# Wider GpSimd additions, later stores and later loads of q and k in an attention and feed-forward kernel

## The chip, the cores and the metric

The kernel runs on one core of one Trainium2 chip, in float32. The metric is the time of one execution on the device in microseconds (us), as the median of several executions. Ratios are the mean time of one kernel's fast runs over that of the other's in the same rounds on the same chip, so they are not quite the ratio of the medians that stand beside them. Where a difference in us is given for an experiment, it is the ratio less one, times 1402 us.

Engine names in the profile: PE is TensorE, PEld its weight loads, DVE is VectorE, ACT is ScalarE, POOL is GpSimd, and SPq is the queue of the SyncE engine, which issues nearly all transfers and does so strictly in order.

## The reference

```python
# attention: batch 8, 12 heads, 448 positions, head size 64
q_n, k_n = rmsnorm(q, g_q), rmsnorm(k, g_k)
scores = matmul(q_n, k_n.T) / sqrt(64)
attn   = softmax(scores)                  # row maximum taken off, 1e-9 added to the sum
x      = matmul(attn, v)                  # -> (3584 tokens, 768)
# feed-forward
h = x @ w_in                              # w_in (768, 2048)
g = maximum(h, 0) ** 2
out = g @ w_out                           # w_out (2048, 768)
```

The two weights arrive as float64. The kernel has to turn them into float32 itself.

## The kernel before

The feed-forward products are done with 7 block products instead of 8 (a Strassen-like scheme), so each pair of weight pieces is first turned into seven blocks: A11, A12, A21, A22 and the sums S1 to S4. These are written to scratch memory in HBM (`w1s`, `w2s`) and read again as blocks `sw` by the products. The two batches that come first have no feed-forward beside them; in this part (`attention_alone`, up to about 134 us) the weights are converted in between. Only this part and the first product after it (134 to 265 us) are touched by the change.

A weight piece goes through one "tick" of four steps. ScalarE and VectorE make the float32 exponent, GpSimd adds the mantissa to it as an integer (`value`) and makes the sums (`total`), and the queue stores the seven blocks:

```python
A11, S2, S1, S3, A12, A22, S4 = range(7)
A21 = 7

def prepare(t):                                  # t: number of the weight piece
    def value(n, half):
        to = ((A11, A12), (A21, A22)) if n < NFC else ((A11, A21), (A12, A22))
        dst = blocks_of(n)[:, to[n % 2][half]]   # 128 x 384
        ...
        nc.gpsimd.tensor_tensor(*[x.bitcast(I32) for x in (dst, low[:, part], eu[:, part])], ALU.add)
    def total(n, dst, x, y, op):
        if there(n) and n % 2:
            nc.gpsimd.tensor_tensor(*[blocks_of(n)[:, i] for i in (dst, x, y)], op)
    ...
    n = t - 3
    if there(n) and n % 2:                       # the store, in the first step
        nc.sync.dma_start(dst.rearrange("k p m -> p k m"), blocks_of(n)[:, 0:7])
    ...
    yield
    ...                                          # second step: ScalarE, VectorE
    yield
    nc.vector.scalar_tensor_tensor(eu, high, 0xC0000000, bits, ALU.bitwise_and, ALU.bitwise_or)
    total(t - 2, S3, A11, A21, ALU.subtract)
    total(t - 2, S4, A12, S2, ALU.subtract)
    value(t - 1, 0)
    yield
    unsigned(t + 1)
    value(t - 1, 1)
    total(t - 1, S1, A21, A22, ALU.add)
    total(t - 1, S2, S1, A11, ALU.subtract)
    load_words(t, t - 1)
    yield
```

One pair of heads in the attention. `norm` squares q and k on ScalarE, sums on VectorE, takes the power -1/2 on GpSimd and multiplies q on GpSimd; `transpose` turns q and k on TensorE; `add_up` adds two tiles of probabilities on VectorE:

```python
def add_up(i, c):
    acc = acc_of(i)[:SP]
    nc.vector.tensor_tensor(acc, probs[i, 0] if c == 1 else acc, probs[i, c], ALU.add)   # 112 x 896

for i in range(NAT):                             # attention_alone, first pair left out
    more = i + 1 < NAT
    if 0 < i < NAT - 3:
        load(i + 3)                              # q and k of the pair after the next two
    scores(i, 0); scores(i, 1)
    if more: transpose(i + 1, 1, 0)              # k, into bank 0
    values(i - 1, (2, 3))
    add_up(i, 1)
    if i + 2 < NAT: norm(i + 2)
    yield
    if more: transpose(i + 1, 0, 0)              # q, into bank 0
    load_v(i + 1)
    yield
    scores(i, 2); scores(i, 3)
    total_of(i - 1); values(i, (0, 1)); finish(i - 1)
    yield
    if added(i) == 3: add_up(i, 2)
    combine_x(i - 1)
    yield
values(i, (2, 3)); total_of(i); finish(i); combine_x(i)
```

At each `yield` of the attention one or two steps of the weights are put in.

Of the kernel before, what the change touches and what calls it, by code (L numbers as in the profile page):

```python
# [9 lines left out]
F32 = mybir.dt.float32  # L10
# [376 lines left out]
def attention_then_ffn_bounded(  # L387
# [100 lines left out]


    A11, S2, S1, S3, A12, A22, S4 = range(7)  # L490
    A21 = 7
    w1s = dram.tile([HF, 7, P, HW], F32, name="w1s")
    w2s = dram.tile([7, HF // 4, P, 4, HW], F32, name="w2s")

# [4 lines left out]
    def words_of(n):  # L499
        place = n % WORDS  # L500
        if place == 0:
            at = BLOCKS * 8 * HW + EXPS * NW
            flat = stage[:, at:at + 2 * NW]
        elif place < 3:
            f = (NFC, HF)[place - 1] - 2
            flat = gT[:, f:f + 2, :].rearrange("p f n -> p (f n)")[:, 0:2 * NW]
        else:
            if (n, "words") not in spare:
                spare[n, "words"] = spare["pool"].tile([P, 2 * NW], F32, tag="words", name="words", bufs=WORDS - 3)
            flat = spare[n, "words"]  # L510
        return flat.bitcast(U32)

    def blocks_of(n):
        at = n // 2 % BLOCKS * 8 * HW
        return stage[:, at:at + 8 * HW].rearrange("p (k m) -> p k m", k=8)
# [27 lines left out]
    def prepare(t):  # L543



        def there(n):
            return 0 <= n < 2 * NFC

        def parts(n):  # L550
            low, high = pairs_of(words_of(n))
            return exponents_of(n), exponents_of(n).bitcast(U32), low, high

        def value(n, half):
            if not there(n):
                return

            to = ((A11, A12), (A21, A22)) if n < NFC else ((A11, A21), (A12, A22))
            dst = blocks_of(n)[:, to[n % 2][half]]
            part = slice(half * HW, (half + 1) * HW)  # L560
            if doubles:
                _, eu, low, _ = parts(n)
                nc.gpsimd.tensor_tensor(*[x.bitcast(I32) for x in (dst, low[:, part], eu[:, part])], ALU.add)  # L563
            else:
                nc.gpsimd.tensor_copy(dst, words_of(n).bitcast(F32)[:, part])

        def total(n, dst, x, y, op):
            if there(n) and n % 2:
                nc.gpsimd.tensor_tensor(*[blocks_of(n)[:, i] for i in (dst, x, y)], op)  # L569

        def unsigned(n):

            if there(n) and doubles:
                e, _, _, high = parts(n)
                nc.scalar.activation(e, high.bitcast(F32), AF.Abs)

        if t == 0:
            unsigned(0)
        n = t - 3
        if there(n) and n % 2:  # L580
            c = n % NFC // 2
            dst = w1s[c] if n < NFC else w2s[:, c // 4, :, c % 4]
            nc.sync.dma_start(dst.rearrange("k p m -> p k m"), blocks_of(n)[:, 0:7])
            written[0] = n + 1
        if there(t) and doubles:
            e, eu, low, high = parts(t)

            nc.vector.tensor_scalar(e, e, 2.0 ** -15, 1.875 * 2.0 ** 16, ALU.max, ALU.min)
        yield
        if there(t) and doubles:  # L590
            nc.scalar.activation(low.bitcast(I32), low, AF.Copy, scale=2.0 ** -29)
            bits = banks.get("bits", eu)
            nc.vector.tensor_scalar(bits, eu, 3, 0x3FFFFFF8, ALU.logical_shift_left, ALU.bitwise_and)
        if t < 3:
            load_words(t, t - 1)
        yield
        if there(t) and doubles:
            nc.vector.scalar_tensor_tensor(eu, high, 0xC0000000, bits, ALU.bitwise_and, ALU.bitwise_or)
        total(t - 2, S3, A11, A21, ALU.subtract)
        total(t - 2, S4, A12, S2, ALU.subtract)  # L600
        value(t - 1, 0)
        yield
        unsigned(t + 1)
        value(t - 1, 1)
        total(t - 1, S1, A21, A22, ALU.add)
        total(t - 1, S2, S1, A11, ALU.subtract)
        load_words(t, t - 1)
        yield

# [45 lines left out]
    def load(i):  # L655
        if i < NAT:
            load_q(nc, qk, q, i)
            load_k(nc, qk, k, i)
            return

        b, h0 = i // NPAIR, 2 * (i % NPAIR)
        for s, src in enumerate((q, k)):
            dst = by_squares(i, 0)[:, s]
            for n in range(4):
                nc.sync.dma_start(dst[n * 32:(n + 1) * 32],
                                  src[b, h0 + n // 2, :, n % 2 * 32:n % 2 * 32 + 32]
                                  .rearrange("(g t) e -> t g e", t=32))
# [65 lines left out]
    def transpose(i, s, n):  # L733

        pt = bank("pt", n)
        for j in range(NJ):
            nc.tensor.transpose(pt[:, j * SP:(j + 1) * SP], normed[i][s][:, j * P:(j + 1) * P], ident[:SP, :SP])  # L737
        if s:
            nc.scalar.copy(qkT[:, i % 2, s], pt)
        else:  # L740
            nc.scalar.activation(qkT[:, i % 2, s], pt, AF.Copy, scale=gains[:, 0:1])
# [58 lines left out]
    def values(i, chunks=range(NJ)):  # L800
        if 0 in chunks:
            pavs[i] = ps_o.tile([P, S], F32, tag="o", name="pav") if i >= NAT or i % 2 == 0 else bank("pav", 1)
        for c in chunks:
            for h in range(2):
                nc.tensor.matmul(pavs[i][h * D:(h + 1) * D, :], vs[i][:, h, c, :], probs[i, c][:, h, :],  # L805
                                 start=(c == 0), stop=(c == NJ - 1))
# [5 lines left out]
    def total_of(i):  # L812


        tots[i] = ps_o.tile([P, S], F32, tag="t", name="tot")
        parts = [acc_of(i)[:SP]] + [probs[i, c] for c in range(added(i), NJ)]
        for n, pr in enumerate(parts):
            for h in range(2):
                nc.tensor.matmul(tots[i][h * D:(h + 1) * D, :], sums["ones"], pr[:, h, :],  # L819
                                 start=(n == 0), stop=(n + 1 == len(parts)))  # L820

    def finish(i):

        b, hp = divmod(i, NPAIR)
        pav, factors = pavs.pop(i), xT[:, b % 2, hp]
        x = factors
        if i < NAT:


            turned, factors = sums["turned"], sums["factors"]  # L830
            few = small.tile([P, S // 32], F32, tag="few", name="few", bufs=1)
            nc.vector.transpose(turned, tots.pop(i))
            nc.vector.reciprocal(few, turned.rearrange("p (g r) -> p g r", r=32)[:, :, 0])
            nc.vector.transpose(factors.rearrange("p (g r) -> p g r", r=32),
                                few.rearrange("p g -> p g ()").to_broadcast([P, S // 32, 32]))

            x = x.rearrange("d (p j) -> d j p", j=NJ)
            pav, factors = (t.rearrange("d (j p) -> d j p", j=NJ) for t in (pav, factors))
        nc.vector.tensor_tensor(x, pav, factors, ALU.mult)
        del vs[i]  # L840
# [15 lines left out]
    def attention_alone():  # L856


        for i in range(NAT):
            more = i + 1 < NAT  # L860
            if 0 < i < NAT - 3:
                load(i + 3)
            scores(i, 0)
            scores(i, 1)
            if i == 0:

                transpose(1, 1, 1)
                scores(0, 2)
                scores(0, 3)
                transpose(1, 0, 0)  # L870
                add_up(0, 1)
                norm(2)
                load_v(1)
                values(0, (0, 1))
                load(3)
                yield
                continue
            if more:
                transpose(i + 1, 1, 0)
            values(i - 1, (2, 3))  # L880
            add_up(i, 1)
            if i + 2 < NAT:
                norm(i + 2)
            elif not more:
                norm(NAT)
                load(NAT + 2)
            yield
            if more:
                transpose(i + 1, 0, 0)
            load_v(i + 1)  # L890
            yield
            scores(i, 2)
            scores(i, 3)
            total_of(i - 1)
            values(i, (0, 1))
            finish(i - 1)
            yield
            if added(i) == 3:
                add_up(i, 2)
            combine_x(i - 1)  # L900
            if NAT <= i + 3 < NAT + 2:
                load(i + 3)
            yield
        values(i, (2, 3))
        total_of(i)
        finish(i)
        combine_x(i)

# [321 lines left out]
```

## Time and profile before

| | before |
|---|---|
| median | 1400.38 us of 3 runs (1400.37 to 1401.83) |
| TensorE busy | 1379.2 of 1399.7 us |
| first product starts (first `pa` after the attention) | 134.21 us |
| second product starts | 264.91 us |
| GpSimd, 56 to 126 us | 68.81 of 70 us busy |
| VectorE, 56 to 126 us | 60.60 of 70 us busy |

The two starts are read from TensorE's timeline. The lines behind the other numbers stand in the prediction.

### The profile page before, as it was taken

Reading aid. Unit: us, or ns where it says so; the run is one execution under the profiler, and the core shown is the slowest. Engines: PE = TensorE matmul, PEld = TensorE weight load, DVE = VectorE, ACT = ScalarE, POOL = GpSimd, SP = SyncE. Lnnn points to the kernel's source line nnn. Section 1 sums busy time; section 2 is a strip of 40 time slices with the busy share of each in tenths; the row PEclk is TensorE's granted clock in tenths of the full one; section 3 lists DMA queues with packets and bytes.
Section 4 is the critical chain, followed back from the end, with each engine's and each line's share of the span. In section 5 each row is a group of like instructions: output and inputs, shape, how many; then the busy total and the mean of one; then the engine's idle time right before and its main releaser. Section 6 shows DMA issues by size and latency. Waiting matters only on the chain.

```text
span 1399.7 us, 14445 instructions
## 1 busy us (share of the span) xinstructions
PE 1379.2 (99%) x4450; PEld 638.5 (46%) x4450; DVE 802.2 (57%) x1398; ACT 419.6 (30%) x621; POOL 581.7 (42%) x400
## 2 busy tenths in 40 slices
PE   8989999999999999999999999999999999999997
PEld 3333455444444454544444455444444445554553
DVE  6889676589876234476777523457777633332111
ACT  7875556432322011233332011233333201110000
POOL 5998877444552123544453122544445302221000
PEclk9999999999999999999999999999999999999999
DMA  9687998545764332344665333344564332334443
GB/s 240 189 229 199 341 384 306 143 97 120 144 121 105 102 90 85 104 113 110 127 130 119 97 94 90 98 106 105 129 126 102 95 101 85 90 87 104 106 111 70
DMA packets 430915, 188.79 MB, mean 135 GB/s; under 512 B 277484, under 2 KB 428780, under 8 KB 430828
## 3 DMA queue, kind: packets, MB, share of 16 engines
q1 hardware_dynamic: 421228, 179.05, 49.8%
q10 hardware_dynamic: 9472, 8.72, 2.3%
q8 instruction: 38, 0.62, 0.2%
q14 instruction: 49, 0.40, 0.1%
q0 software_dynamic: 128, 0.00, 0.0%
HBM read 154.54 MB, written 33.16 MB: 134 GB/s over the span
## 4 chain that ended last, share of the span: by engine, by line
PE 93%; POOL 3%; DVE 1%; DMA 1%; ACT 1%; issue 1%; ACTq 0%; POOLq 0%
PE ps L1047 37%; PE sc L749 10%; PE pd L1000 10%; PE pa L1000 10%; PE pc L1000 10%; PE pav L805 9%; PE pb L1000 5%; PE tot L819 1%; POOL rstd L697 1%; POOL gC L563 1%; DMA sw<-w1s 1%; POOL gC L569 1%; PE pt L737 0%; ACT gT L754 0%; POOL qk L699 0%
## 5 line engine op out<-in xcount | busy, mean ns | idle before, releaser
L1047 PE MATMUL ps<-gT,sw 128*128 128x448 f32 x768 | 299.2, 543 | 0.8 <-POOL gT L977 0.8
L719 POOL TENSOR_TENSOR half<-half,mhalf 128x28 f32<-128x28 f32 x36 | 173.6, 4822 | 266.9 <-DVE half L718 226.8
L1047 PE MATMUL ps<-gC,sw 128*128 128x448 f32 x576 | 225.2, 543 | 0.0
L977 POOL TENSOR_TENSOR gT<-gT 128x448 f32<-128x448 f32 x96 | 94.9, 990 | 309.9 <-ACT gT L973 309.9
L1047 PEld LDWEIGHTS ps<-gT,sw 128*128 128x128 f32 x768 | 144.1, 190 | 150.7 <-issue 147.0
L756 ACT ACTIVATE pr<-sc 112x896 f32<-112x896 f32 x120 | 104.7, 914 | 293.4 <-PE sc L749 184.9
L749 PE MATMUL sc<-qkT 64*112 64x448 f32 x768 | 170.6, 563 | 0.9 <-ACT qkT L383 0.8
L1047 PEld LDWEIGHTS ps<-gC,sw 128*128 128x128 f32 x576 | 108.2, 190 | 112.1 <-issue 110.8
L1000 PE MATMUL pa<-xT,sw 128*128 128x448 f32 x384 | 154.9, 540 | 0.0
L973 ACT ACTIVATE gT<-gT 128x448 f32<-128x448 f32 x96 | 55.3, 577 | 310.1 <-DVE gT L1015 310.0
L749 PEld LDWEIGHTS sc<-qkT 64*112 64x112 f32 x768 | 61.2, 173 | 97.9 <-issue 81.3
L1000 PEld LDWEIGHTS pa<-xT,sw 128*128 128x128 f32 x384 | 73.0, 190 | 71.6 <-issue 70.3
L805 PE MATMUL pav<-pr,vt 112*64 112x448 f32 x480 | 100.2, 547 | 0.0
L721 POOL TENSOR_TENSOR qk<-qk,half 128x448 f32<-128x448 f32 x72 | 81.3, 1150 | 2.8
L764 DVE TENSOR_TENSOR acc<-acc,pr 112x896 f32<-112x896 f32 x60 | 68.2, 1136 | 21.0 <-ACT pr L756 18.5
L1000 PE MATMUL pb<-xC,sw 128*128 128x448 f32 x192 | 77.6, 540 | 1.5 <-issue 1.5
L1000 PE MATMUL pd<-xT,sw 128*128 128x448 f32 x192 | 77.9, 542 | 0.0
L1000 PE MATMUL pc<-xC,sw 128*128 128x448 f32 x192 | 77.5, 540 | 0.2 <-DMA sw<-w1s 0.2
L1000 PE MATMUL pd<-xC,sw 128*128 128x448 f32 x192 | 77.5, 540 | 0.0
L1000 PE MATMUL pc<-xT,sw 128*128 128x448 f32 x192 | 77.4, 539 | 0.0
L1015 DVE TENSOR_TENSOR gT<-z,pd 128x448 f32<-128x448 f32 x32 | 19.8, 620 | 99.7 <-PE pd L1000 99.7
L569 POOL TENSOR_TENSOR gC<-gC 128x384 f32<-128x384 f32 x64 | 72.8, 1157 | 2.5
(120 smaller groups left out, 1551.0 us busy)
## 6 DMA issues: line engine op xcount, KB each, us to landing
sw<-w1s SPq DMA_DIRECT2D x224, 192.0 KB, 2.3
sw<-w2s SPq DMA_DIRECT2D x168, 256.0 KB, 3.3
w1s<-gC SPq DMA_DIRECT2D x8, 1344.0 KB, 7.5
w2s<-gC SPq DMA_DIRECT2D x8, 1344.0 KB, 7.6
out_dram<-osb SPq DMA_DIRECT2D x184, 56.0 KB, 1.9
qk<-in_q_dram SPq DMA_DIRECT2D x144, 56.0 KB, 3.0
qk<-in_k_dram SPq DMA_DIRECT2D x144, 56.0 KB, 2.9
vt<-in_v_dram SPq DMA_DIRECT2D x72, 112.0 KB, 2.9
```

Source lines behind the costliest of these rows:

```text
L569: nc.gpsimd.tensor_tensor(*[blocks_of(n)[:, i] for i in (dst, x, y)], op)
L719: nc.gpsimd.tensor_tensor(half, half, mhalf, ALU.pow)
L721: nc.gpsimd.tensor_tensor(qkn[:, s], raw[:, s], half[:, s * NG:(s + 1) * NG].rearrange("p g -> p g ()").to_broadcast([P, NG, 32]), ALU.mult)
L749: nc.tensor.matmul(sc[:, h, 0:S], qkT[rows, at, 1, c * SP:(c + 1) * SP], qkT[rows, at, 0, :], start=True, stop=True)
L756: nc.scalar.activation(pr, sc[:, :, 0:S], AF.Exp)
L764: nc.vector.tensor_tensor(acc, probs[i, 0] if c == 1 else acc, probs[i, c], ALU.add)
L805: nc.tensor.matmul(pavs[i][h * D:(h + 1) * D, :], vs[i][:, h, c, :], probs[i, c][:, h, :], start=(c == 0), stop=(c == NJ - 1))
L973: nc.scalar.activation(g, src, AF.Relu)
L977: nc.gpsimd.tensor_tensor(g, g, g, ALU.mult)
L1000: nc.tensor.matmul(ps, stream[n + i][:, c], rhs[:, c], start=first and c == 0, stop=c == HC - 1, skip_group_check=not first)
L1015: add(g, x, ps, ALU.add)
L1047: nc.tensor.matmul(ps, stream[n][:, c % 4], rhs_of[i][:, c], start=c == 0, stop=c == HF - 1)
```

## The change

Its intent: relieve GpSimd, which is full in the attention, by doing two equal additions in one operation of twice the width; and keep the queue of transfers from standing still, by storing later and by loading q and k behind the values of the pair. Two smaller parts: in odd pairs q is transposed into another PSUM bank than k, and the last pair's total is computed ahead of its last quarter of values.

```diff
-    A21 = 7
+    A21 = -1
...
+        def put(op, *places):
+            lone = any(len(x) == 2 and x[1] <= x[0] for _, x in places)
+            for take in [slice(0, 1), slice(1, 2)] if lone else [slice(0, 2)]:
+                op(*[of[:, x[take][0]:x[take][-1] + 1:max(x[take][-1] - x[take][0], 1)] for of, x in places])
...
+            put(add, blocks(n, *to[n % 2]), *[(x, [0, 1]) for x in halves])
...
-                nc.gpsimd.tensor_tensor(*[blocks_of(n)[:, i] for i in (dst, x, y)], op)
+                put(lambda *z: nc.gpsimd.tensor_tensor(*z, op), *[blocks(n, *i) for i in (dst, x, y)])
...
-        n = t - 3                                   (the store: from here, the first step ...)
...
         yield
+        n = t - 3                                   (... to here, the third step)
+        if there(n) and n % 2:
+            nc.sync.dma_start(dst.rearrange("k p m -> p k m"), blocks_of(n)[:, 1:8])
...
-        total(t - 2, S3, A11, A21, ALU.subtract)
-        total(t - 2, S4, A12, S2, ALU.subtract)
-        value(t - 1, 0)
+        total(t - 2, (S3, S4), (A11, A12), (A21, S2), ALU.subtract)
         yield
+        value(t - 1)
         unsigned(t + 1)
-        value(t - 1, 1)
...
-            if 0 < i < NAT - 3:
-                load(i + 3)
             scores(i, 0)
...
-                transpose(i + 1, 0, 0)
+                transpose(i + 1, 0, i % 2)
...
             finish(i - 1)
+            if i + 3 < NAT:
+                load(i + 3)
...
-        values(i, (2, 3))
+        values(i, (2,))
         total_of(i)
+        values(i, (3,))
```

More of the change, by code (lines that the diff above doesn't have):

```diff
@@ L552, in parts, with blocks, value @@
             return exponents_of(n), exponents_of(n).bitcast(U32), low, high
-        def value(n, half):
+        def put(op, *places):
+            lone = any(len(x) == 2 and x[1] <= x[0] for _, x in places)
+            for take in [slice(0, 1), slice(1, 2)] if lone else [slice(0, 2)]:
+                op(*[of[:, x[take][0]:x[take][-1] + 1:max(x[take][-1] - x[take][0], 1)] for of, x in places])
+        def blocks(n, *which):
+            return blocks_of(n), [1 + i for i in which]
+        def value(n):
             if not there(n):
@@ L558, in value, with add @@
             to = ((A11, A12), (A21, A22)) if n < NFC else ((A11, A21), (A12, A22))
-            dst = blocks_of(n)[:, to[n % 2][half]]
-            part = slice(half * HW, (half + 1) * HW)
+            halves = [x.rearrange("p (two m) -> p two m", two=2) for x in
+                      ((parts(n)[2], parts(n)[1]) if doubles else (words_of(n),))]
             if doubles:
-                _, eu, low, _ = parts(n)
-                nc.gpsimd.tensor_tensor(*[x.bitcast(I32) for x in (dst, low[:, part], eu[:, part])], ALU.add)
-            else:
-                nc.gpsimd.tensor_copy(dst, words_of(n).bitcast(F32)[:, part])
+                def add(*x):
+                    nc.gpsimd.tensor_tensor(*[y.bitcast(I32) for y in x], ALU.add)
+            else:
+                def add(dst, src):
+                    nc.gpsimd.tensor_copy(dst, src.bitcast(F32))
+            put(add, blocks(n, *to[n % 2]), *[(x, [0, 1]) for x in halves])
         def total(n, dst, x, y, op):
             if there(n) and n % 2:
-                nc.gpsimd.tensor_tensor(*[blocks_of(n)[:, i] for i in (dst, x, y)], op)
+                put(lambda *z: nc.gpsimd.tensor_tensor(*z, op), *[blocks(n, *i) for i in (dst, x, y)])
         def unsigned(n):
@@ L578, in prepare @@
             unsigned(0)
-        n = t - 3
-        if there(n) and n % 2:
-            c = n % NFC // 2
-            dst = w1s[c] if n < NFC else w2s[:, c // 4, :, c % 4]
-            nc.sync.dma_start(dst.rearrange("k p m -> p k m"), blocks_of(n)[:, 0:7])
-            written[0] = n + 1
         if there(t) and doubles:
@@ L596, in prepare @@
         yield
+        n = t - 3
+        if there(n) and n % 2:
+            c = n % NFC // 2
+            dst = w1s[c] if n < NFC else w2s[:, c // 4, :, c % 4]
+            nc.sync.dma_start(dst.rearrange("k p m -> p k m"), blocks_of(n)[:, 1:8])
+            written[0] = n + 1
         if there(t) and doubles:
             nc.vector.scalar_tensor_tensor(eu, high, 0xC0000000, bits, ALU.bitwise_and, ALU.bitwise_or)
-        total(t - 2, S3, A11, A21, ALU.subtract)
-        total(t - 2, S4, A12, S2, ALU.subtract)
-        value(t - 1, 0)
+        total(t - 2, (S3, S4), (A11, A12), (A21, S2), ALU.subtract)
         yield
+        value(t - 1)
         unsigned(t + 1)
-        value(t - 1, 1)
-        total(t - 1, S1, A21, A22, ALU.add)
-        total(t - 1, S2, S1, A11, ALU.subtract)
+        total(t - 1, (S1,), (A21,), (A22,), ALU.add)
+        total(t - 1, (S2,), (S1,), (A11,), ALU.subtract)
         load_words(t, t - 1)
```

## The prediction

> **What bounds the kernel now.** I read the busy shares first, then the chain of work that ended last, then a table by stage, and last the timelines of the engines where TensorE has gaps. The busy shares on the page:
>
> ```profile
> PE 1379.2 (99%) x4450; PEld 638.5 (46%) x4450; DVE 802.2 (57%) x1398; ACT 419.6 (30%) x621; POOL 581.7 (42%) x400
> ```
>
> TensorE is busy 1379.2 of 1399.7 us. Nothing in the diff touches the number, shape or operands of its matmuls, so the change can win only what TensorE idles, about 20.5 us or 1.5%. That already rules out a 2% gain by filling gaps; it would take 28 us. GpSimd's 42% is an average over unlike stages, so I looked where the gaps lie. Busy time by stage (the columns are PE, PEld, DVE, ACT, POOL, granted clock, share of the DMA engines, GB/s):
>
> ```profile
> 0.00:20.00 20.00, 15.66 (x66) 6.64 (x66) 9.53 (x24) 14.95 (x26) 12.02 (x16) 1.00 0.81 211
> 140.00:180.00 40.00, 39.81 (x106) 19.61 (x105) 27.84 (x36) 22.23 (x34) 33.84 (x32) 1.00 1.00 351
> 180.00:220.00 40.00, 40.00 (x108) 20.12 (x107) 29.96 (x36) 26.90 (x43) 32.70 (x33) 1.00 1.02 374
> 1050.00:1400.00 350.00, 341.89 (x973) 167.31 (x971) 120.31 (x208) 42.38 (x66) 61.58 (x50) 1.00 0.38 95
> 56.00:126.00 70.00, 65.47 (x338) 24.91 (x336) 60.60 (x77) 53.96 (x90) 68.81 (x44) 1.00 0.84 227
> 126.00:140.00 14.00, 11.73 (x51) 4.54 (x48) 13.46 (x24) 2.08 (x4) 9.65 (x6) 1.00 0.74 177
> 20.00:56.00 36.00, 34.64 (x172) 13.44 (x174) 31.03 (x42) 29.46 (x50) 27.76 (x17) 0.95 0.74 206
> ```
>
> TensorE's idle time: 4.3 us in the first 20, 1.4 from 20 to 56, 4.5 from 56 to 126, 2.3 from 126 to 140, 0.2 to 180, and 8.1 at the very end (the last outputs on their way out). Start and end are not touched. What is left is the attention without a feed-forward beside it, up to 140 us: 8.2 us. From 56 to 126 us GpSimd is the full engine, 68.81 of 70 us, while TensorE needs 65.47. From 126 to 140 it is VectorE, 13.46 of 14. The gaps one by one, from TensorE's timeline (start, duration, idle before it, what released it):
>
> ```profile
> 21.36 0.60 PE L737 MATMUL pt<-ident,qk 112*128 112x112 f32 x4 [1.91 <-ACT qkT L739]
> ...
> 72.13 0.60 PE L737 MATMUL pt<-ident,qk 112*128 112x112 f32 x4 [0.50 <-POOL qk L699]
> 82.91 0.60 PE L737 MATMUL pt<-ident,qk 112*128 112x112 f32 x4 [1.45 <-POOL qk L699]
> 95.34 0.60 PE L737 MATMUL pt<-ident,qk 112*128 112x112 f32 x4 [2.25 <-POOL qk L699]
> 115.08 0.61 PE L737 MATMUL pt<-ident,qk 112*128 112x112 f32 x4 [0.22 <-POOL qk L699]
> 131.80 2.48 PE L819 MATMUL tot<-gT,ones 112*64 112x448 f32 x12 [0.82 <-DVE gT L832]
> 138.18 2.49 PE L1000 MATMUL pb<-xC,sw 128*128 128x448 f32 x6 [1.45 <-issue]
> ```
>
> Four waits for the normalised q of the next pair (0.50 + 1.45 + 2.25 + 0.22 = 4.4 us) are GpSimd's. The chain of waits agrees: between 76 and 115 us it runs through GpSimd's power (L697), multiplication (L699), values (L563) and block sums (L569). From GpSimd's timeline, one pair of heads:
>
> ```profile
> 82.81 1.01 POOL L563 TENSOR_TENSOR gC<-words,gC 128x384 int32<-128x384 int32 x1
> 83.91 4.73 POOL L569 TENSOR_TENSOR gC<-gC 128x384 f32<-128x384 f32 x4
> 88.59 1.99 POOL L563 TENSOR_TENSOR gC<-words,gC 128x384 int32<-128x384 int32 x2
> 90.55 3.62 POOL L697 TENSOR_TENSOR rstd<-rstd,mhalf 112x16 f32<-112x16 f32 x1
> 94.25 1.04 POOL L699 TENSOR_TENSOR qk<-qk,rstd 112x512 f32<-112x512 f32 x1
> ```
>
> The reader is to see that seven preparations of weights stand in GpSimd's queue ahead of the power, and that TensorE's transposition at 95.34 starts as soon as L699 ends. The weights are not urgent here; they are only ahead in the queue.
>
> **The Trainium skill.** "GPSIMD Engine Reference", section 3.1, gives a two-input operation 4497 ns for 2048 elements (2.2 ns an element) and names two software dispatch hops per instruction. 384 elements would be 0.84 us by that; undisturbed pairs here take 1.99 to 2.00 us for two, so roughly 0.16 us of each operation isn't proportional to its size. "SBUF — State Buffer", section "Who interferes with whom", says that a VectorE instruction with two SBUF inputs contends with a GpSimd instruction that reads SBUF. The trace agrees in direction: a block sum averages 1329 ns in the first 140 us, where VectorE is most loaded, and (72.8 - 26.3) / 44 = 1057 ns later. Wider operations do not take this away. "DMA: Bandwidth & Descriptors", section "Queues, rings and completion order", says that descriptors on one ring are consumed in order. Here one block of w1 issued at 147.47, just behind a 1344 KB store at 146.10, took 9.4 us to land against a median of 2.3.
>
> **The change part by part.**
>
> 1. Wider additions. Before, each of 32 weight pieces has two values (64 operations) and each of 16 pairs of pieces four block sums (64). After, all 16 pieces of the first weight and 8 of the second get one value of 768 elements; the other 8 keep two, since their destinations are in descending order: 16 + 8 + 16 = 40. S3 and S4 become one operation: 48 sums. So 128 operations become 88. The elements are the same, so each of the 40 saves only the fixed part. From 0.16 (above) and the gaps between instructions of 0.02 to 0.07 us in the chain, I take 0.18 us: 7 us of GpSimd in all, an estimate. Only the full stretch counts: from 61 to 126 us its timeline has 16 values and 16 sums, thus 8 + 4 merges, 12 x 0.18 = 2.2 us. They come off a queue that TensorE waits 4.4 us for. In the first product (134 to 260 us) TensorE is full, so the other merges win nothing. Part 1: **-2.2 us**.
>
> 2. Another bank for q's transposition in odd pairs. The wait of 1.91 us at 21.36 was for ScalarE to empty the bank that k's transposition had filled; in pair 1 the other bank is free. But q itself must be normalised, and ScalarE's exponentials are full there, so the next scores may wait instead. I take half: **-1.0 us**.
>
> 3. Total ahead of the last quarter of values in the last pair. The total waited for VectorE (L832 at 131.1 to 131.7), whose queue is full, so it can hardly start sooner; the quarter (0.8 us of TensorE) then fills part of the 1.45 us before pb instead of standing before the total. The gap moves rather than closes: **-0.2 us**.
>
> 4. Stores half a step later, loads of q and k behind the values. The queue that issues transfers waited long, but mostly for nothing that TensorE needed at once:
>
> ```profile
> SPq L583 <- POOL gC L569: 37.5, 5, 10.7
> SPq L315 <- POOL qk L699: 16.7, 5, 5.6
> ```
>
> Later stores shorten the first wait, so loads behind them go out sooner; the loads of q and k themselves are moved back by half a pair (a pair takes about 9.7 us). Their lead was 8 to 12 us; I count about 8 after, with landing times of 3 to 5 us. ScalarE has slack (54 of 70 us), so being late by 1 or 2 us is mostly absorbed, as at 83.22, where it waited 1.97 us for k and TensorE waited for GpSimd anyway. In the first product the DMA engines are full (1.00 and 1.02), and a store that meets a load of words there could starve TensorE: **+0.5 us** for both.
>
> Sum: -2.2 - 1.0 - 0.2 + 0.5 = -2.9 us; with 1400.4 this gives about 1397.5.
>
> **The rivals.** (a) Relieving GpSimd closes all four of its waits, because the shorter queue lets the power pass in front more often than the saved time tells: TensorE's 65.47 us in that stretch then is the bound. For it: no other engine is over 61 of 70. With the whole 1.9 and 0.8 us of parts 2 and 3 this is 1400.4 - 7.1 = 1393.3. (b) The wait moves: k arrives late, ScalarE's square holds up the copy of q and the exponentials, or VectorE (60.6 of 70, 13.46 of 14 at the end) becomes the bound; the gaps stay and the time is 1399 to 1401. Against it: VectorE's work isn't changed. (c) A transfer becomes the wait in the first product, where 192 KB blocks have to pass stores of 1344 KB. For it: the 9.4 us landing, with only 0.2 us of TensorE's wait so far; against: five blocks are loaded ahead, about 11 us at 2.26 us each. It would cost 1 to 3 us: 1398 to 1402. (d) Bigger GpSimd operations block VectorE for longer at a time; same sum of blocking, so little.
>
> **Range and chances.** The low end is rival (a) in full, 1393.3; the high end is no gain and some of (c), 1401.0. The middle is 1397.5. A 2% step is 28 us, more than all of TensorE's idle time, and nothing in the diff adds 28 us to it, so within 2% gets 0.98.
>
> **What would show it.** In the profile of the changed kernel: the same 1379 us of TensorE; 40 fewer GpSimd operations, those of 768 elements at about 1.83 us undisturbed; the waits of TensorE for L699 down from 4.4 to about 2.2 us; the wait of 1.91 us at 21 us halved; GpSimd below 68 of 70 in its stretch; the queue's wait at the stores well under 37.5 us. Wrong would be: merged operations at 2.0 us (no fixed part to save), new waits of TensorE for ScalarE or blocks of w1, or new gaps after 260 us, where nothing should change.

## The result

The changed kernel takes 1414.15 us (1413.81 to 1415.36, 4 runs); the kernel before, in the same rounds, 1401.11 us (1400.37 to 1403.38). The ratio is 1.0092, with a 95% interval of 1.0074 to 1.0109. It is within 2%, but slower by about 13 us, and outside the range that was predicted.

The busy shares on the page of the changed kernel:

```profile
PE 1385.4 (98%) x4450; PEld 639.3 (45%) x4450; DVE 824.8 (58%) x1398; ACT 420.3 (30%) x621; POOL 574.0 (41%) x360
```

GpSimd has its 40 operations fewer and works 7.7 us less. But VectorE, with the same 1398 operations, is busy 22.6 us longer, and TensorE, with the same 4450 matmuls, 6.2 us longer. The largest single part of VectorE's increase is its sums of probabilities (20 to 140 us, before and changed; busy us, mean ns):

```profile
L764 DVE TENSOR_TENSOR gT<-gT 112x896 f32<-112x896 f32 x16 | 20.9, 1312 | 3.2 <-ACT gT L754 3.2
L775 DVE TENSOR_TENSOR gT<-gT 112x896 f32<-112x896 f32 x16 | 34.8, 2182 | 0.0
```

The stages of the changed kernel (same columns as before):

```profile
20.00:56.00 36.00, 34.14 (x176) 12.84 (x174) 35.32 (x41) 31.74 (x53) 24.61 (x13) 1.00 0.75 213
56.00:126.00 70.00, 60.54 (x294) 23.02 (x291) 66.39 (x68) 45.44 (x75) 60.95 (x29) 0.93 0.74 201
```

GpSimd is no longer full in its stretch (60.95 of 70); VectorE now is (66.39). TensorE gets less done there, not more: 60.54 us against 65.47. Its timeline has these waits:

```profile
63.40 0.60 PE L748 MATMUL pt<-ident,qk 112*128 112x112 f32 x4 [1.61 <-POOL qk L710]
...
75.15 0.60 PE L748 MATMUL pt<-ident,qk 112*128 112x112 f32 x4 [1.67 <-POOL qk L710]
...
86.37 0.61 PE L748 MATMUL pt<-ident,qk 112*128 112x112 f32 x4 [1.88 <-POOL qk L710]
...
102.39 1.01 PE L748 MATMUL pt<-ident,qk 112*128 112x112 f32 x4 [4.29 <-POOL qk L710]
...
141.26 3.95 PE L830 MATMUL tot<-gT,ones 112*64 112x448 f32 x12 [1.80 <-DVE gT L843]
...
160.47 2.49 PE L1012 MATMUL pd<-xC,sw 128*128 128x448 f32 x6 [2.81 <-DMA sw<-w1s]
```

The wait for GpSimd's normalised q, which the change was to shorten, more than doubled, from 4.4 to 9.5 us (1.61 + 1.67 + 1.88 + 4.29). The wait at 21 us for the bank is gone. A wait of 2.81 us for a block of the first weight is new. And some matmuls take twice as long: the total at 141.26 takes 3.95 us where the same work took 2.48 before. The granted clock, as a share of TensorE's full clock, shows why (window, TensorE busy, clock, then the DMA columns):

```profile
98.00:102.00 4.00, 0.10 (x2) 0.90 0.84 273
102.00:106.00 4.00, 3.61 (x12) 0.50 0.56 129
...
142.00:146.00 4.00, 4.00 (x14) 0.57 0.00 0
```

After some of its waits TensorE runs at half its clock. The trace's clock record, finer than these windows of 4 us, has only full and half clock, and half clock comes in stretches of 3.41 us: one from 9.0, one from 87.5, two from 101.2 and one from 142.1 us. The kernel before has one, from 22.3 us, after its wait of 1.91 us at 21 us. The Trainium skill has this in "TensorE: Matmul & The Clock Gate", Part 1: the clock is halved after an idle window of some 3.4 us. The length of a stretch agrees, and so does the wait of 4.29 us, followed by 0.50; but the shorter wait of 1.80 us at 141 us was followed by 0.57 as well.

What sets these two apart from waits that cost no clock can be read from the traces. In each trace the stretches at half clock lie whole multiples of 3.41 us apart, so the time from 8 to 290 us can be cut into such stretches, and TensorE's idle time in each (between matmul records, whose ends are modelled) can be set against the clock of the next. In the 17 traces told of here, all 28 stretches at full clock with 1.80 us or more of idle time were followed by half clock, 3 of the 15 with 1.58 to 1.72 us, and none of the 1308 with less: about half a stretch is the limit. So a wait counts by how it lies. The 1.80 us at 141 us lie in one stretch; the 2.81 us at 160 us are split into 1.53 and 1.28, and the clock stays full.

The first product starts at 146.12 us (134.21 before), the second at 278.12 (264.91). From there to the end it is 1134.6 us, against 1134.8 before. So the whole loss is made before the second product: 11.9 us in the attention and 1.3 in the first product.

### The profile page after: what moved, and what is told of

It is laid out like the page before. It is cut to its first block, busy times and chain, and to the rows that moved or that the text cites. A ratio compares the mean times of both kernels' runs of the same rounds, so it can differ in the third digit from the quotient of the medians.

```text
span 1412.7 us, 14405 instructions
## 1 busy us (share of the span) xinstructions
PE 1385.4 (98%) x4450; PEld 639.3 (45%) x4450; DVE 824.8 (58%) x1398; ACT 420.3 (30%) x621; POOL 574.0 (41%) x360
## 4 chain that ended last, share of the span: by engine, by line
PE 89%; POOL 5%; issue 2%; DVE 1%; DMA 1%; ACT 1%; SPq 0%; POOLq 0%; ACTq 0%; DVEq 0%
PE ps L1059 36%; PE pd L1012 10%; PE pa L1012 10%; PE pc L1012 10%; PE sc L760 9%; PE pav L816 8%; PE pb L1012 5%; POOL rstd L708 2%; POOL gC L581 1%; POOL qk L710 1%; POOL gC L573 1%; DMA words<-in_moe_w_out_dram 0%; PE tot L830 0%; DMA w1s<-gC 0%; ACT gT L765 0%
## 5 line engine op out<-in xcount | busy, mean ns | idle before, releaser
L760 PE MATMUL sc<-qkT 64*112 64x448 f32 x768 | 173.7, 571 | 0.9 <-ACT qkT L383 0.8
L581 POOL TENSOR_TENSOR gC<-gC 128x384 f32<-128x384 f32 (+1 forms) x48 | 70.2, 1462 | 3.5
```

The lines of the kernel that those rows point to most:

```text
L581: put(lambda *z: nc.gpsimd.tensor_tensor(*z, op), *[blocks(n, *i) for i in (dst, x, y)])
L760: nc.tensor.matmul(sc[:, h, 0:S], qkT[rows, at, 1, c * SP:(c + 1) * SP], qkT[rows, at, 0, :], start=True, stop=True)
```

## The experiments

Three theories stood at first. **A**: the wide operations keep VectorE off the port that it shares with GpSimd, so VectorE's sums, and with them the norms, come late. **B**: q and k are loaded too late. **C**: it is the order, since both values of a piece now stand in one step with the sums. All kernels gave correct results.

| kernel | ratio (95% interval) | first product at | second at | VectorE's sum of probabilities, mean / longest ns | at half clock, us |
|---|---|---|---|---|---|
| before | | 134.21 | 264.91 | 1312 / 1956 | 3.4 |
| changed | 1.0092 (1.0074 to 1.0109) | 146.12 | 278.12 | 2182 / 5511 | 17.1 |
| e1 changed, narrow | 1.0075 (1.0056 to 1.0095) | 141.69 | 272.89 | 1657 / 1933 | 3.4 |
| e2 changed, early loads | 1.0067 (1.0051 to 1.0084) | 144.35 | 274.90 | 2176 / 5510 | 13.7 |
| e3 before, wide | 1.0049 (1.0033 to 1.0066) | 140.49 | 272.18 | 2163 / 5508 | 6.8 |
| e4 before, late loads | 1.0085 (1.0069 to 1.0102) | 148.79 | 277.55 | 1483 / 1936 | 17.1 |
| e5 as e3, narrow | 1.0005 (0.9986 to 1.0024) | 134.34 | 265.05 | 1319 / 1936 | 3.4 |
| e6 before, later stores | 1.0038 (1.0013 to 1.0063) | 133.95 | 270.34 | 1531 / 1923 | 10.2 |
| e7 as e3, wide halved | 1.0003 (0.9986 to 1.0020) | 136.16 | 267.80 | 1327 / 1953 | 6.8 |
| e8 changed, total back | 1.0085 (1.0068 to 1.0102) | 144.87 | 277.63 | 2379 / 5524 | 10.2 |
| e9 before, bank | 0.9995 (0.9983 to 1.0008) | 132.80 | 263.35 | 1491 / 1935 | 0 |
| e10 before, bank, 44 steps | 1.0004 (0.9992 to 1.0017) | 132.13 | 267.69 | 1606 / 1935 | 3.4 |
| e11 as e3, wide values | 1.0034 (1.0016 to 1.0052) | 139.51 | 271.54 | 1751 / 3749 | 10.2 |
| e12 as e3, wide sums | 1.0042 (1.0025 to 1.0059) | 139.62 | 269.89 | 1669 / 3710 | 10.2 |
| e13 before, bank and total | 0.9994 (0.9976 to 1.0012) | 133.66 | 263.90 | 1502 / 1930 | 0 |
| e14 changed, narrow, early loads | 1.0028 (1.0010 to 1.0045) | 136.08 | 270.61 | 1516 / 1955 | 6.8 |
| e15 before, late loads, later stores | 1.0078 (1.0060 to 1.0096) | 139.35 | 275.13 | 1649 / 1930 | 10.2 |

The starts, the sums (20 to 140 us) and the time at half clock (before 290 us) are from one profiled execution of each kernel.

### Which part loses: e1 to e4

e1 splits every wide addition of the changed kernel again and leaves all else:

```diff
-            lone = any(len(x) == 2 and x[1] <= x[0] for _, x in places)
+            lone = len(places[0][1]) == 2
```

> The changed kernel with every GpSimd addition of two blocks split back into two of 384 elements; order, stores, loads, bank and last total stay as changed. Theory A (wide GpSimd operations shut VectorE's additions of two SBUF operands out until they are over, so the norms come late): the slow part is gone, 1398 to 1403 us, and VectorE's sum of probabilities falls from a mean of 2182 ns back to about 1300 ns with none over 2.2 us. Theory B (loads of q and k too late): stays at 1411 to 1415. Theory C (values and sums now stand in one step, whatever their width): stays at 1411 to 1415.

Measured: 1411.92 us, ratio 1.0075. The longest sum of probabilities is back at 1933 ns, as A has it (the mean, 1657 ns, only in part), but the time is not back: 2.4 us of 13 are regained, which is within the noise. ScalarE's wait for k rose to 14.2 us.

e2 moves only the loads back in the changed kernel:

```diff
+            if 0 < i < NAT - 3:
+                load(i + 3)
             scores(i, 0)
...
             finish(i - 1)
-            if i + 3 < NAT:
-                load(i + 3)
```

> The changed kernel with only the loads of q and k moved back to the start of the pair. Theory A: 1409 to 1414, VectorE's sum of probabilities still above 2 us on average, ScalarE's wait for k down from 8.9 us. Theory B: 1398 to 1402. Theory C: 1409 to 1415.

Measured: 1411.85 us, ratio 1.0067; ScalarE's wait for k fell to 2.0 us. That is the number of theories A and C, and it excludes B as the only cause.

e3 is the kernel before with only the wide additions, and with the block order and the single step for values that they need. Its diff is the first half of the change.

> The kernel before with only the wide additions (and the block order and the single step of the values that they need); stores, loads, bank and last total as before. Theory A: the loss is here, 1408 to 1415, with sums of probabilities above 2 us on average and single ones of 4 to 5.5 us. Theory B: 1398 to 1402. Theory C: 1408 to 1415 as well; it is told from A by the first run.

Measured: 1408.94 us, ratio 1.0049: 6.9 us of loss from this part alone, with single sums of up to 5508 ns. TensorE's waits for q rise from 4.4 to 7.3 us.

e4 is the kernel before with only the loads moved:

```diff
-            if 0 < i < NAT - 3:
-                load(i + 3)
             scores(i, 0)
...
             finish(i - 1)
+            if i + 3 < NAT:
+                load(i + 3)
```

> The kernel before with only the loads of q and k moved behind the pair's values. Theory A: 1399 to 1403, as GpSimd's backlog hides a late k. Theory B: 1408 to 1415 with ScalarE waiting 6 us or more for k. Theory C: 1399 to 1403.

Measured: 1414.61 us, ratio 1.0085, with 19.8 us of ScalarE's waits for k. Here theory B has it. So A or C and B are both at work, and neither of the first three theories was the whole. The lines of e4 show what a late load runs into. Its queue:

```profile
76.89 0.38 SPq L583 DMA_DIRECT2D w1s<-gC  x1
77.36 0.51 SPq L315 DMA_DIRECT2D qk<-in_q_dram  x1
77.97 2.57 SPq L325 DMA_DIRECT2D qk<-in_k_dram  x2
```

The store `w1s<-gC` waited until 76.89 for GpSimd's last sum (13.9 us, by the queue's own waits), and the loads of q and k, now behind it in the queue, waited with it. ScalarE and TensorE then:

```profile
85.24 1.06 ACT L693 ACTIVATE qk<-qk 112x1024 f32<-112x1024 f32 x1 [12.90 <-DMA qk<-in_k_dram]
```

```profile
88.70 3.33 PE L749 MATMUL sc<-qkT 64*112 64x448 f32 x8 [9.09 <-ACT gT L754]
```

The square of q and k stands in front of the exponentials in ScalarE's queue, so TensorE lost 9.09 us at one place, and its scores then ran at half clock (0.50 from 88 to 92 us; 3.33 us instead of 1.76). In the kernel before, the load that this square needs had been issued in front of the store that held up the queue: at 61.30, while its own store waited until 74.88.

### What in the wide additions: e5, e7, e11, e12

e5 is e3 with narrow operations (the diff of e1), so only order and place of the blocks are left.

> The kernel with the wide additions alone (1408.9 us), but with every wide addition split back into two of 384 elements: what is left of it is the order (both values in one step) and the place of the blocks. If the width costs the time (theory A): 1400 to 1404 us and VectorE's sum of probabilities at 1300 to 1700 ns on average, none above 2.5 us. If the order does (theory C): 1407 to 1411.

Measured: 1402.27 us, ratio 1.0005. Order and place cost nothing; theory C is out, the width costs.

e7 keeps the access pattern of the wide operations, two blocks at once, but cuts each into two of 2 x 192 elements:

```diff
-                op(*[of[...] for of, x in places])
+                views = [of[...] for of, x in places]
+                wide = len(places[0][1][take]) == 2
+                for part in [slice(0, HW // 2), slice(HW // 2, HW)] if wide else [slice(0, HW)]:
+                    op(*[v[:, :, part] for v in views])
```

> The kernel with the wide additions alone, each wide one split into two that still go over both blocks, 2 x 192 elements each, so as many instructions as before the change with the access pattern of the wide ones. If the length of one instruction shuts VectorE out: 1400 to 1404 us and sums of probabilities at 1300 to 1700 ns on average. If the pattern of two rows does: 1407 to 1411 and above 2 us on average.

Measured: 1402.82 us, ratio 1.0003, sums at 1327 ns on average. It is the length of one operation, not its pattern.

How this happens shows in the merged timeline of VectorE and GpSimd at the same place of the two kernels. First e5, narrow:

```profile
49.18 3.28 POOL L581 TENSOR_TENSOR gC<-gC 128x384 f32<-128x384 f32 x2
...
49.52 1.62 DVE L774 TENSOR_TENSOR gT<-gT 112x896 f32<-112x896 f32 x1
...
52.42 3.16 POOL L573 TENSOR_TENSOR gC<-gT,gC 128x384 int32<-128x384 int32 x2
...
52.80 1.90 DVE L774 TENSOR_TENSOR gT<-gT 112x896 f32<-112x896 f32 x1
```

Then e3, wide:

```profile
47.87 1.04 POOL L709 TENSOR_TENSOR qk<-qk,rstd 112x512 f32<-112x512 f32 x1
...
48.64 4.81 DVE L774 TENSOR_TENSOR gT<-gT 112x896 f32<-112x896 f32 x1
...
48.87 1.82 POOL L581 TENSOR_TENSOR gC<-gC 128x768 f32<-128x768 f32 x1
...
50.64 1.86 POOL L573 TENSOR_TENSOR gC<-gT,gC 128x768 int32<-128x768 int32 x1
...
56.94 3.77 POOL L707 TENSOR_TENSOR rstd<-rstd,mhalf 112x16 f32<-112x16 f32 x1 [4.44 <-DVE rstd L705]
```

An undisturbed sum of probabilities takes 1.08 us. In e5 it waits for the rest of one narrow operation and then goes in between two; it is GpSimd that waits meanwhile (3.28 us for two operations of 1.0). In e3 it waits through the multiplication, the wide sum and the wide value, and starts only when GpSimd has run dry at 52.5: 4.81 us. Everything behind it in VectorE's queue is late, also the reduction that the next norm needs. At 56.94 GpSimd, which was to be relieved, has stood idle for 4.44 us waiting for VectorE. The Trainium skill's "SBUF — State Buffer", section "Who interferes with whom", gives the first half of this: a VectorE instruction with two SBUF inputs contends with a GpSimd instruction that reads SBUF. What these lines add is when VectorE gets its turn: in e5 before the next narrow operation, in e3 not before a wide one, not even between the multiplication and the wide sum. The other traces agree. In all 17, sums of probabilities that took over 1.3 us stood waiting 327 times while GpSimd went from one operation to the next. Where the next one had at most 512 elements, VectorE got in, 290 times of 290. Where it had 768, GpSimd went on 33 times of 37; in the other 4, GpSimd itself had paused for 0.08 us, for its own previous sum.

e11 makes only the values wide, e12 only the sums S3 and S4, both from e3:

```diff
 # e11
-            lone = any(len(x) == 2 and x[1] <= x[0] for _, x in places)
+            lone = any(len(x) == 2 and x[1] <= x[0] for _, x in places) or places[0][1] == [1 + S3, 1 + S4]
 # e12
+            lone = len(places[0][1]) == 2 and places[0][1] != [1 + S3, 1 + S4]
```

> The kernel with the wide additions alone (1408.9 us), its wide block sums split again, so only values are wide (11 of them before the first product). If each wide instruction shuts VectorE out by its own length: about two thirds of the loss, 1404 to 1408 us, sums of probabilities at 1700 to 2100 ns on average. If only wide sums do: 1400 to 1403.

> The kernel with the wide additions alone, its values split again, so only S3 and S4 are wide (5 instructions before the first product). If each wide instruction shuts VectorE out by its own length: about a third of the loss, 1402 to 1405 us, sums of probabilities at 1400 to 1800 ns on average. If only wide sums do: 1406 to 1410.

Measured: 1407.35 (ratio 1.0034) and 1407.45 us (1.0042). The values behave as expected. The sums are a miss: five wide instructions cost about as much as eleven, 5.9 us. Most of it in that trace is one wait of TensorE, 5.72 us for q at 98.72, and the half clock around and after it. So the loss does not go by the number of wide operations. The clock is part of the reason: e11 and e12 run 10.2 us at half clock, e3 6.8 and e5 3.4. How five wide sums lead to the long wait is not shown: between 77 and 107 us of e12 no sum of probabilities is passed over for a wide operation.

### The later stores: e6

Only the store of the kernel before is moved from the first to the third step of the tick, as in the change's diff.

> The kernel before with only the stores half a step later. If stores are harmless: 1400 to 1404 us, the issuing queue waits less than 37.5 us for block sums. If a later store delays what stands behind it in the queue: 1405 to 1412, with ScalarE's wait for k above 6 us.

Measured: 1406.69 us, ratio 1.0038. The first product starts at 133.95 us, as early as before, so the attention isn't hurt, and ScalarE's wait for k stays at 2.0 us: the number of the second alternative came for another reason. The loss is in the first product. TensorE of e6:

```profile
150.75 4.82 PE L1000 MATMUL pd<-xC,sw 128*128 128x448 f32 x6 [3.58 <-DMA sw<-w1s]
```

And e6's queue:

```profile
136.64 1.88 SPq L665 DMA_DIRECT2D qk<-in_q_dram  x4
...
140.65 0.48 SPq L595 DMA_DIRECT2D w1s<-gC  x1
141.17 0.56 SPq L535 DMA_DIRECT2D gT<-in_moe_w_out_dram  x1
...
144.36 2.36 SPq L646 DMA_DIRECT2D sw<-w1s  x4
```

The kernel before:

```profile
123.44 0.38 SPq L583 DMA_DIRECT2D w1s<-gC  x1
...
136.90 1.88 SPq L665 DMA_DIRECT2D qk<-in_q_dram  x4
...
142.49 3.05 SPq L646 DMA_DIRECT2D sw<-w1s  x4
```

The loads at 136.64 wait for GpSimd (L721), and those at 136.90 before do so too; the queue stands still for it for 11.6 us in e6 and for 1.4 before. Before, the store had been issued at 123.44, ahead of them. Half a step later it falls behind them and goes out at 140.65, with 1344 KB in front of the four blocks that TensorE needs next, which go out at 144.36 instead of 142.49. TensorE waits 3.58 us for one, and that matmul group then takes 4.82 us instead of 2.42 at a granted clock of 0.50 (150 to 154 us).

### The small parts: e8, e9, e13

e8 puts the last pair's total back behind all its values in the changed kernel.

> The changed kernel with only the last pair's total put back behind all its values. If moving it lengthened TensorE's wait there enough for its clock to be halved (granted clock 0.57 from 142 to 146 us): 1410 to 1412.5 us, 1.5 to 3.5 below the changed kernel, with a granted clock of 1.00 around that total. If the move is neutral as predicted: 1413.5 to 1415.

Measured: 1413.79 us, ratio 1.0085. The idea that this move had halved TensorE's clock was wrong: the clock falls to 0.60 there in e8 as well.

e9 has only the other bank in the kernel before (`transpose(i + 1, 0, i % 2)`), timed in 5 rounds:

> The kernel before with only the other bank for q's transposition in odd pairs. As predicted: 1399.5 to 1400.5 us, about 1 us below the kernel before. If the wait only moves to the next total, which needs VectorE's sum: 1400.5 to 1402.5 and a new wait of 0.5 to 1.5 us for that sum.

Measured: 1401.31 us, ratio 0.9995 (0.9983 to 1.0008). The wait of 1.91 us at 21 us is gone (0.40 is left, for the scores), but 1.51 us come back at 60.26 as a wait for GpSimd's q. So the waits before the first product are about as long as before (7.06 us from 20 us on, against 7.15). The first product starts 1.4 us earlier in its trace because no wait in it halves the clock: before, the 3.41 us from 22.3 us at half clock cost about 1.7 us (an estimate, half of 3.41). The time lies in the range of the second alternative, though the new wait is for another engine; it doesn't separate e9 from the kernel before.

e13 has the bank and the total:

> The kernel before with only the two small parts, the other bank and the last pair's total ahead of its last values. If the loss of the changed kernel is all in wide additions, late loads and late stores: 1399.5 to 1402.5 us, level with the kernel before. If moving the total costs: 1403 to 1405.

Measured: 1400.65 us, ratio 0.9994. The total waits 1.58 us instead of 0.82, and pb 0.74 instead of 1.45: the gap moved and stayed the same size, as predicted.

### A version that was to beat both: e10

e10 is e9 with less weight work beside the attention:

```diff
-    EARLY, ALL = 4 * 13, 4 * (2 * NFC + 3)
+    EARLY, ALL = 4 * 11, 4 * (2 * NFC + 3)
```

> A version meant to beat both: the kernel before with that bank and with 44 instead of 52 steps of preparing weights beside the first attention, so that two pieces fewer go through GpSimd there and more in the first product, where TensorE is full. If GpSimd's queue is what TensorE waits for: waits for the normalised q fall from 4.4 to under 2 us and the time to 1395 to 1399. If the first product's transfers can't take the rest: 1400 to 1406 with new waits for blocks of w1 or w2.

Measured: 1402.86 us, ratio 1.0004: no gain. The first product starts earlier (132.13) but loses it again to waits for blocks of w1 (1.05, 0.64 and 0.88 us) and for VectorE. The waits for q did not fall either (5.4 us). No version was found that beats the kernel before beyond the noise.

### How the parts add up: e14, e15

Alone, the wide additions cost 6.9, the late loads 11.9 and the later stores 5.3 us, 24 together; the changed kernel loses 13.

> The changed kernel without wide additions and without late loads: later stores, bank and total are left. If the parts stand alone as measured so far: 1404 to 1408 us as with the later stores alone (1406.7), the attention as fast as before (the first product starting by 135 us) and one wait of 2 to 4 us for a block of w1. If the parts only hurt in company: 1400 to 1403.

e14 (the diffs of e1 and e2 together) took 1406.70 us, ratio 1.0028: the number of the later stores alone, with one wait of 3.43 us for a block of w1. So the stores cost about the same within the changed kernel (3.9 us against 5.3, within the noise). The first product starts at 136.08 us, later than the 135 expected.

> The kernel before with late loads and later stores. If a late load costs because it stands behind a store that waits for GpSimd, later stores shorten that: ScalarE's longest wait for k falls from 12.9 to under 7 us and the time to 1407 to 1411, below the late loads alone (1414.6), though the later stores alone cost 5. If the two add up: 1417 to 1421.

e15 (e4 and e6 together) took 1412.35 us, ratio 1.0078: less than the late loads alone, but 1.35 us above the range expected. ScalarE's waits for k fell from 19.8 to 10.3 us and the longest from 12.9 to 4.5. The two don't add up: with later stores in place, the late loads cost 5.6 us more (10.9 less 5.3) instead of 11.9. The store's place explains it: in e15 the loads of q and k behind the values at 61.10 and 62.86 were issued in front of the store at 76.82, not behind it.

The steps can be put in a row, within the width of the intervals (2 to 3 us each): later stores 5.3 (e6), with late loads 10.9 (e15), with bank, total and order 10.5 (e1), with wide additions 12.9 (changed).

## Why the prediction was wrong

**The bound.** Right for what could be won and from the second product on, where the time is unchanged; the step stays within 2%. It was no bound on what could be lost: "the same 1379 us of TensorE" became 1385.4 for the same 4450 matmuls, and the later stores lose their time after 140 us, in the first product.

**Step 1, wide additions.** Its cost was about right. Undisturbed values take 1.84 to 1.86 us (1.83 predicted), which saves about 0.15 us each (0.18 predicted), and GpSimd's sum fell by 7.7 us (7 predicted; 40 times 0.15 us would be 6). The 0.16 us on the way there were partly luck: 0.84 us for 384 elements is an estimate that takes all of the page's time for 2048 as proportional. The effect had the wrong sign: not -2.2 us but +6.9 alone, and about +2.4 (not clear of the noise) on top of the other parts. TensorE's waits for q were to fall from 4.4 to about 2.2 us; they rose to 7.3 in e3. The sentence that failed is rival (d): "Bigger GpSimd operations block VectorE for longer at a time; same sum of blocking, so little." The sum of blocking was not the same. The 16 sums of probabilities took 34.8 us together instead of 20.9, the longest went from 1956 to 5511 ns, and VectorE, which the prediction had noted at 60.6 of 70 us, had no room for it. Rival (b) named VectorE as the possible bound, but held against it that "VectorE's work isn't changed"; its work isn't, its waiting for GpSimd is.

**Step 2, the bank.** -0.7 us measured (interval -2.4 to +1.1) against -1.0, but the nearness is luck. The wait at 21 us went and nearly all of it came back later; what e9's trace gains is the clock, which the prediction's own table shows (0.95 from 20 to 56 us) and its text does not read.

**Step 3, the total.** Right: the gap moved, and e13 is level with e9.

**Step 4, stores and loads.** Put at +0.5 us for both; the later stores alone cost 5.3, and the late loads 5.6 more. Two statements failed. The lead of the loads was counted by their place in the program ("about 8 after"), without the queue's order: a store that waits for GpSimd holds back whatever stands behind it, 13.9 us in e4. And "later stores shorten the first wait" was true (37.5 us to 23.9), but a store that comes later also falls behind the next wait in the queue, and then in front of blocks that are needed at once. Rival (c) had this in kind (blocks of w1 that have to pass a store of 1344 KB, 1 to 3 us). The wait is 2.81 us in the changed kernel and 3.58 in e6, but (c) missed the half clock that comes on top.

**What the prediction lacked.** After some waits TensorE's clock is halved. In the changed kernel the windows of 4 us that start at 86, 90, 102, 106 and 142 us have granted clocks of 0.69, 0.88, 0.50, 0.75 and 0.57; by busy time times the missing share they lose 1.1 + 0.5 + 1.8 + 1.0 + 1.7 = 6.1 us (an estimate), nearly all of the 6.2 us that TensorE is busy longer. Both kernels also have one stretch of 3.41 us at half clock before 30 us (from 9.0 and from 22.3 us). So the loss of 13 us is about half waiting and half clock.

**Left open.** Why VectorE gets its turn before a GpSimd operation of 512 elements and not before one of 768; no run shows the arbitration itself, or a size in between. And what decides on the clock where 1.58 to 1.72 us of a stretch are idle.

## What to carry to other kernels

Fewer and larger operations on GpSimd save about 0.15 us each, but beside a nearly full VectorE with two SBUF inputs they can cost several times that, since VectorE may get no turn before them: check how long the other engine's operations become, not only how long one's own are. When a transfer is moved in an in-order queue, follow what stands in front of it there and what that waits for; its place in the program says little about when it starts. And where the critical engine is 99% busy, as here, each part of a change should be tried alone before they are put together.

## What the Trainium skill lacked or had wrong

- "SBUF — State Buffer", section "Who interferes with whom", says that VectorE instructions with two SBUF inputs contend with GpSimd, and that the order of issue, not the shape of the operation, decides who blocks, but not who comes next when an operation ends. Here that went by size: a waiting VectorE addition of 1.08 us got in before GpSimd operations of up to 512 elements (1.62 and 1.90 us), but not before those of 768 that followed without a pause (4.81 and up to 5.51 us).
- "GPSIMD Engine Reference", section 3.1, gives no number for GpSimd's cost per instruction, and section 2.1 only "tens of cycles" for one part of it. Two integer additions of 384 elements took 1.99 to 2.00 us, one of 768 took 1.85: about 0.15 us for one instruction.
- "TensorE: Matmul & The Clock Gate", Part 1, speaks of an idle window of some 3.4 us (and, without a length, of short idle spells that come often). Granted clocks of 0.57 and 0.60 followed waits of only 1.80 and 2.07 us (the changed kernel and e8, 142 to 146 us), though a wait of 2.25 us in the kernel before, split over two stretches of 3.41 us, left it at 1.00. In 17 traces 1.80 us of idle time in one stretch was always enough, 28 times of 28.
- No page has the cost of an in-order queue whose head waits: one store held back loads of q and k by 13.9 us (e4), and a store moved by half a step kept TensorE waiting 3.58 us for a block (e6).
